# One region of fixed order, index copies behind the first expert's rows, longer planned times for two steps

## The chip, the cores and the metric

The kernel runs on one core of a Trainium2 chip. The metric is the device time of one execution in microseconds, as the median of several runs. The core's engines are TensorE (PE, with its weight loads shown apart as PEld), VectorE (DVE), ScalarE (ACT), GpSimd (POOL) and SyncE (SP); DMA queues carry the transfers.

## What is computed

Attention without a softmax, an RMS norm, and then a mixture of 8 experts in which every token goes to the one expert with the largest logit, up to a capacity. Cut to what matters:

```python
kv = np.einsum('bhsd,bhse->bhde', k, v)              # 8 batches, 8 heads, 576 x 64
out = np.einsum('bhsd,bhde->bhse', q, kv)
x = out / np.sqrt(np.mean(out * out, -1, keepdims=True) + 1e-06) * g_norm   # 4608 tokens x 512
logits = x @ w_gate
expert_idx, gate_w = argmax(logits), softmax(logits)[expert_idx]
# token i goes to the next free slot of its expert, if one is left (cap 1152)
h = np.maximum(np.einsum('ecd,edf->ecf', disp, w1), 0.0)   # 512 -> 1024
y = np.einsum('ecf,efd->ecd', h, w2)                       # 1024 -> 512
out[i] = gate_w[i] * y[expert_idx[i], pos[i]]
```

## The kernel before

**Precision.** Each product is made of three fp16 products: rows and weights are split into a high part and a low part (`xs`, `w1h`/`w1l`, `w2h`/`w2l`, `hh`/`hl`), and high x high, high x low and low x high are added up in fp32.

**Stages.** The attention takes the batches one after the other; its rows go to a table in DRAM, `x_dram` (written at L1050 and L1052), and a routing step ranks each token within its expert. After a few batches the most frequent expert is picked, its weights are loaded, and 384 of its rows (`EARLY`) are worked on beside the rest of the attention. When all batches are through, ten last matmuls (`tab`, L1031, from `rhs`, L1024) finish the table of slots; `read_table` (L1112) turns it into the indices `gidx_tab` (where a slot's row is read) and `sidx_tab` (where its result is written), and `rank_experts` orders the experts by their number of tokens. Then the experts follow by rank, 0 to 7, with `BUDGET` = 704, 672, 640, 624, 592, 576, 560, 544 rows; for rank 0 the 320 rows behind the first 384 are left.

**One expert.** SP loads w1 and w2 in four parts each (`raw`, L341). VectorE takes the largest absolute value of each eighth (`am`, L357); through two small matmuls (`pt_max`, L370 and L377) the largest of all comes back to VectorE, which makes a power of two of it in six small steps (`bmax` to `sg`, L381 to L386: the op `scale`). ScalarE writes the high parts (L391), VectorE the low ones (L397). VectorE copies the expert's six columns of the index table (`slots`, L660; its register load L665, copies `gi` and `si` L669: the op `cut`). GpSimd gathers rows by them, 128 at a time (`xg`, L453, an indirect DMA); `xm` (L461) applies the norm, `gt` (L466) reads the gate weight. Rank 0's rows are turned by TensorE (`xp`, L472), and ScalarE and VectorE write the high and low part of `xs` (L703, L480); from rank 1 on the parts are written to `pair` (L486, L490) and turned by DMA (L494). GEMM1 (`hp`, L557) makes 8 blocks of 128 hidden units, each in one of two PSUM buffers; ScalarE takes the relu (`hh`, L562), VectorE the rest (`hl`, L565), which frees the buffer. `ysc` (L594, L595: the op `scaled`) holds the scale of each result row. GEMM2 (`op` or `yp`, L604) adds up 24 matmuls for a tile of 128 rows, ScalarE writes it out scaled (`ysb`, L629), GpSimd scatters it to DRAM (L634).

**Order.** The kernel doesn't issue in program order. A list scheduler (`Plan`, L107) takes ops with a planned time on an engine, what they depend on, what buffers they take, and a key; at each step it places on the engine that is free first the op with the lowest key among those that are ready. `plan.emit()` then calls them by planned start. So a planned time moves no instruction by itself: it changes when the scheduler thinks that an engine is free. There are two plans. The first holds the attention, the routing and the early 384 rows. The second (from L1525) holds the rest: `weights` (L1540) with `scale` planned at 1.1, `rows_beside` (L1588) with `cut` at 0.4, `products` (L1622) with `scaled` at 1.2, and the loop over ranks at L1678. Each plan is emitted in a region of its own of `manual_schedule`, which keeps each engine's instructions in the order of emission; between the two, at L1344 and L1691, the framework's own scheduler is free to put instructions of one region ahead of those of the other:

Of the kernel before, what the change touches and what calls it, by code (L numbers as in the profile page):

```python
# [26 lines left out]
MANUAL = ("PE", "Activation", "DVE", "Pool", "SP")  # L27
# [17 lines left out]
FIRST = -50.0  # L45
KEY = 10.0
EARLY_TILES = 1
ROWS = 0.0
# [41 lines left out]
class Plan:  # L90
# [5 lines left out]
    def op(self, ways, fn, deps=(), key=0.0, takes=(), uses=()):  # L96

        ways = [ways] if isinstance(ways[0], str) else list(ways)
        o = Op(ways, fn, [d for d in deps if d is not None], list(takes), key)
        for h in takes + uses if isinstance(takes, tuple) and isinstance(uses, tuple) else list(takes) + list(uses):  # L100
            h.users.append(o)
        self.ops.append(o)
        return o
# [56 lines left out]
def attention_moe_kernel(  # L160
# [534 lines left out]
    op = plan.op  # L695
# [420 lines left out]
    early = {}  # L1116
# [224 lines left out]
    order = ExitStack()  # L1341
    order.enter_context(tc.manual_schedule(engines={getattr(mybir.EngineType, e) for e in MANUAL}))
    plan.emit()
    order.close()  # L1344
    actx.close()


# [178 lines left out]
    op = plan.op  # L1526
# [8 lines left out]
    def weights(r, key, after):  # L1535

        ws, sets, zs, holds = wsets[r % 2], [], [], []
        for i in range(2):
            f, z = split_weight(i, ws, (raw1, raw2)[i])
# [8 lines left out]
            for p in range(4):  # L1548
                o = op(("S", 0.43), lambda e, i=i, p=p, regs=regs: load(e, i, p, regs),
                       [regs.get("op"), early["rank"]] + after + (early["free"][p] if r == 1 and i == 0 else []), key,  # L1550
                       (raws[p],))
# [12 lines left out]
            x = new("x")  # L1564
# [5 lines left out]
            o = op(("V", 0.3), lambda e, f=f: f["most"](), tops, FIRST)  # L1570
            o.late = LATE[1] if r > 1 else 0.0
            o = op(("T", 0.12), across, [o], FIRST, (x,))
# [1 line left out]
            o.late = LATE[2] if r > 1 else 0.0  # L1574
            o = op(("T", 0.31), lambda e, f=f, x=x: f["back"](x.t[:, 0:1]), [o], FIRST, (), (x,))
            ew = new(f"e{i}")
            o = op(("V", 1.1), lambda e, f=f, x=x: f["scale"](x.t[:, 0:1]), [o], FIRST, (ew,), (x,))
            zs.append((z, o, ew))
            highs, lows = [], []
            for p in range(8):  # L1580
# [4 lines left out]
            holds.append(hold)  # L1585
        return sets, zs, holds

    def rows_beside(r, key):  # L1588

        hold, sl, st = new("xs"), new("slots"), {}  # L1590

        def cut(e):
            st["gi"], st["si"] = slots(mo, perm_i[0:1, 1, r:r + 1])

        cut_ = op(("V", 0.4), cut, [early["rank"]], key, (sl,))
        n = len(spans(0, BUDGET[r]))
        gates, turned, first, sent = [], [], None, []
        for i in range(n):
            xg, xm, pair = new("xg"), new("xm"), new("pair")

            def fetch(e, i=i):
                if i == 0:
                    st["x"] = Rows(mo, st["gi"], 0, BUDGET[r], BM)
                st["x"].fetch(i)

            o = op(("P", 1.2), fetch, [cut_, first], key, (hold, xg), (sl,))
            first = first or o
            o = op(("D", 0.85), None, [o], key, (), (xg,))
            o.late = 9 if r > 1 else 1.2
            a = op([("P", 1.28), ("V", 0.6)] if r < 3 else ("P", 1.28), lambda e, i=i: st["x"].norm(i, either[e]), [o], key + 1,  # L1610
                   (xm,), (xg,))
            gates.append(op(("V", 0.07), lambda e, i=i: st["x"].gate(i), [o], key + 1, (), (xg, hold)))
            a = op(("A", 0.52), lambda e, i=i: st["x"].pair_high(i), [a], key + 1, (pair,), (xm, hold))
            a = op([("P", 1.37), ("V", 0.66)] if r < 3 else ("P", 1.37), lambda e, i=i: st["x"].pair_low(i, either[e]), [a],
                   key + 1, (), (xm, pair, hold))
            a = op(("S", 1.45), lambda e, i=i: st["x"].pair_turn(i), [a], key + 1, (), (pair, hold))
            sent.append(a)
            turned.append(op(("D", 0.95), None, [a], key + 1, (), (pair, hold)))
            turned[-1].late = 9 if r > 1 else 1
        return st, hold, sl, gates, turned, sent  # L1620

    def products(r, x, xh, xl, gates, xs_hold, si, sl_hold, sets, zs, w_holds, s0, s1):  # L1622
# [32 lines left out]
        def scales(e):  # L1655
            st["g2"] = Gemm2(mo, wsets[r % 2], st["g1"], x().gt, si(), s0, s1)
            st["g2"].scales(y_scale(*[z["e"] for z, _, _ in zs]))

        scaled = op(("V", 1.2), scales, hh[:1] + gates + [o for _, o, _ in zs], urgent, (),
                    (xs_hold, *[x for _, _, x in zs]))  # L1660
        second(r, st, hh, hl, sets and sets[1], scaled, hid, w_holds[1], sl_hold, s0, s1, y_bank)
        return hh
# [5 lines left out]
    def moved(e):  # L1668
# [6 lines left out]
                                              mo, None, lambda: psx.tile([P, 512], F32, tag="x", name="xp"), new("xs"), BM)  # L1675
    args = (lambda st=st: st["rows"], xh, xl, gates, xs_hold, lambda: early["si0"], Hold(None), None, zs, w_holds, EARLY,
            BUDGET[0])
    for r in range(E):  # L1678
        hh = products(r, *args)
        key = KEY * r  # L1680
        if r + 1 < E:
            sets, zs, w_holds = weights(r + 1, key + 1, [] if r > 1 else sent)
            st, xs_hold, sl, gates, turned, sent = rows_beside(r + 1, key + ROWS)
            args = (lambda st=st: st["x"], turned, turned, gates, xs_hold, lambda st=st: st["si"], sl, sets, zs, w_holds, 0,
                    BUDGET[r + 1])
        else:
            op(("P", 9.0), lambda e: nc.gpsimd.drain(), hh[:2], key)
            steps, o = plan_rest(), hh[0]
            for _ in range(60):
                o = op(("V", 0.2), lambda e: next(steps, None), [o], key + 1)  # L1690
    order = ExitStack()  # L1691
    order.enter_context(tc.manual_schedule(engines={getattr(mybir.EngineType, e) for e in MANUAL}))
    plan.emit()
    order.close()
    rest(**table)
# [31 lines left out]
```

## Time and profile before

| what | value |
|---|---|
| median of 3 runs | 574.98 us (573.97 to 575.07) |
| profiled execution | 569.37 us |
| its span, from the first to the last instruction | 567.6 us |
| mean granted TensorE clock | 0.982 |
| TensorE busy | 528.5 us, 93% of the span, 4490 matmuls |
| VectorE busy | 386.8 us, 68% |
| ScalarE busy | 252.6 us, 45% |
| GpSimd busy | 198.9 us, 35% |
| DMA | 102.71 MB, mean 181 GB/s |

The shares are means over stages. In the profile's 40 slices of 14.2 us TensorE is at nine tenths or more nearly everywhere from 184 us on; below that are the first slice (4 tenths), six within the attention (7 or 8), and the two from 156 to 184 us (7), which hold the step from the attention to the experts. So the table says that TensorE is the engine to look at, and the timeline of the slices that are not full says what it waits for. Durations come from the one profiled execution; the span has no launch in it, which is why its own time is 1.8 us longer.

### The profile page before, as it was taken

To read this page: it belongs to the slowest core of one execution; us is meant where nothing else is said; L and a number is where in the kernel's file an instruction comes from. 1 tells how busy PE (TensorE), PEld (TensorE's weight loads), DVE (VectorE), ACT (ScalarE), POOL (GpSimd) and SP (SyncE) were. 2 spreads that over 40 slices of the span, in tenths; PEclk is the share of its full clock that TensorE was granted. 3 is DMA by queue.
4 is the path that set the end of the run, shared out by engine and by line. 5 is a ranking of instruction groups with operands and counts; after the bars stand their busy time and mean duration, and the time that the engine had idled before them with its cause. 6 is when DMAs were issued, how large, how long until landed. Compare 5 with 4: busy or idle time off the path is not lost.

```text
span 567.6 us, 11867 instructions
## 1 busy us (share of the span) xinstructions
PE 528.5 (93%) x4490; PEld 364.6 (64%) x4490; DVE 386.8 (68%) x1072; ACT 252.6 (45%) x490; POOL 198.9 (35%) x244
## 2 busy tenths in 40 slices
PE   4999987978877999999999999999999999999995
PEld 4988876965434576546754674677477558648843
DVE  4387897999838999998999677395848607203800
ACT  1687663886102662655625524253353426212201
POOL 3003335245132471355506431742452375021011
PEclk9999995999999999999999999999999999999998
DMA  8999999662149589699667565583665342010000
GB/s 279 332 357 357 377 383 381 210 257 95 52 150 360 113 250 261 154 308 180 198 160 239 163 153 164 143 172 101 206 159 122 79 102 57 18 55 22 2 37 33
DMA packets 81905, 102.71 MB, mean 181 GB/s; under 512 B 39148, under 2 KB 63724, under 8 KB 80818
## 3 DMA queue, kind: packets, MB, share of 16 engines
q1 hardware_dynamic: 74240, 70.50, 43.3%
q0 software_dynamic: 7584, 31.38, 16.7%
q8 instruction: 37, 0.61, 0.4%
q14 instruction: 26, 0.21, 0.1%
q10 hardware_dynamic: 18, 0.02, 0.0%
HBM read 73.20 MB, written 20.68 MB: 165 GB/s over the span
## 4 chain that ended last, share of the span: by engine, by line
issue 32%; PE 29%; DMA 16%; POOL 13%; DVE 8%; ACT 1%; POOLq 1%; SPq 0%; DVEq 0%
PE hp L557 10%; PE yp L604 9%; DMA v_sb<-in_v_dram 4%; POOL out_dram L634 4%; DMA k_sb<-in_k_dram 4%; POOL pair L490 4%; DMA q_sb<-in_q_dram 3%; POOL xg L453 3%; PE op L823 2%; POOL xm L461 2%; DMA xs<-pair 2%; DVE w1l L397 2%; PE op L557 2%; DMA raw<-in_moe_w_dram 2%; DMA xg<-x_dram,gi 1%
## 5 line engine op out<-in xcount | busy, mean ns | idle before, releaser
L557 PE MATMUL hp<-xs,w1h 128*128 128x320 f16 (+6 forms) x960 | 134.2, 292 | 2.4 <-DVE gt L466 1.2
L557 PEld LDWEIGHTS <-w1h 128*128 128x128 f16 x1024 | 99.4, 98 | 40.0 <-issue 7.3
L634 POOL DMA_INDIRECT out_dram<-ysb,si x42 | 42.9, 1020 | 153.8 <-ACT ysb L629 150.7
L604 PEld LDWEIGHTS <-hh 128*128 128x128 f16 x560 | 54.4, 98 | 63.7 <-issue 1.6
L562 ACT ACTIVATE hh<-hp 128x320 f16<-128x320 f32 (+7 forms) x64 | 41.0, 640 | 108.5 <-PE hp L557 108.5
L357 DVE TENSOR_REDUCE am<-raw 128x1 f32<-128x512 f32 x120 | 75.6, 673 | 4.1 <-DMA raw<-in_moe_w_dram 4.1
L629 ACT ACTIVATE ysb<-yp,ysc 128x512 f32<-128x512 f32 (+5 forms) x41 | 28.1, 685 | 99.9 <-PE yp L604 93.6
L557 PE MATMUL hp<-xs,w1l 128*128 128x320 f16 (+6 forms) x480 | 72.0, 292 | 0.0
L565 DVE SCALAR_TENSOR_TENSOR hl<-hp,hh 128x320 f16<-128x320 f32 (+7 forms) x64 | 47.4, 741 | 32.8 <-ACT hh L562 32.7
L604 PE MATMUL yp<-w2h,hh 128*128 128x512 f16 x272 | 65.3, 379 | 0.8 <-ACT ysb L629 0.8
L604 PE MATMUL yp<-w2l,hh 128*128 128x512 f16 x272 | 65.4, 383 | 0.0
L604 PE MATMUL yp<-w2h,hl 128*128 128x512 f16 x272 | 65.0, 381 | 0.0
L453 POOL DMA_INDIRECT xg<-x_dram,gi x42 | 44.0, 1048 | 49.6 <-DVE gt L466 13.0
L557 PEld LDWEIGHTS <-w1l 128*128 128x128 f16 x512 | 49.8, 98 | 16.3
L823 PE MATMUL op<-kv_bd,qt 128*128 128x144 f32 x320 | 53.0, 301 | 3.5 <-ACT qt L703 2.7
L397 DVE SCALAR_TENSOR_TENSOR w2l<-raw,sw,w2h 128x512 f16<-128x512 f32 x64 | 51.6, 848 | 5.2 <-ACT w2h L391 5.2
L619 DVE COPY yt<-yp 128x256 f32<-128x256 f32 (+4 forms) x7 | 2.9, 412 | 73.4 <-PE yp L613 63.8
L490 POOL TENSOR_TENSOR pair<-xm,pair 128x512 f16<-128x512 f32 (+5 forms) x26 | 34.0, 1308 | 50.3 <-ACT pair L486 50.1
L397 DVE SCALAR_TENSOR_TENSOR w1l<-raw,sg,w1h 128x512 f16<-128x512 f32 x64 | 50.1, 816 | 1.5 <-ACT w1h L391 1.5
L604 PEld LDWEIGHTS <-hl 128*128 128x128 f16 x280 | 27.3, 98 | 32.2 <-issue 1.1
L823 PEld LDWEIGHTS op<-kv_bd,qt 128*128 128x128 f32 x320 | 44.1, 196 | 5.6 <-ACT qt L703 2.9
L391 ACT ACTIVATE w2h<-raw,sw 128x512 f16<-128x512 f32 x62 | 39.7, 710 | 8.1 <-PE yp L613 7.2
(247 smaller groups left out, 698.0 us busy)
## 6 DMA issues: line engine op xcount, KB each, us to landing
raw<-in_moe_w_dram SPq DMA_DIRECT2D x64, 512.0 KB, 5.4
x_dram<-o_sb POOLq DMA_DIRECT2D x8, 720.0 KB, 6.5
k_sb<-in_k_dram SPq DMA_DIRECT2D x16, 320.0 KB, 6.6
v_sb<-in_v_dram SPq DMA_DIRECT2D x16, 320.0 KB, 7.9
q_sb<-in_q_dram SPq DMA_DIRECT2D x16, 320.0 KB, 6.9
x_dram<-o_sb POOLq DMA_DIRECT2D x8, 576.0 KB, 7.4
k_sb<-in_k_dram SPq DMA_DIRECT2D x16, 256.0 KB
v_sb<-in_v_dram SPq DMA_DIRECT2D x16, 256.0 KB, 4.5
```

Source lines behind the costliest of these rows:

```text
L357: nc.vector.tensor_reduce(out=am()[:, p:p + 1], in_=raw[:, sl(p)], axis=AX.X, op=ALU.max, apply_absolute_value=True)
L391: nc.scalar.activation(wh[:, sl(p)], raw[:, sl(p)], AF.Copy, scale=z["s"])
L397: nc.vector.scalar_tensor_tensor(out=wl[:, sl(p)], in0=raw[:, sl(p)], scalar=z["s"], in1=wh[:, sl(p)], op0=ALU.mult, op1=ALU.subtract)
L453: nc.gpsimd.indirect_dma_start(out=self.xg[i][0:n], out_offset=None, in_=x_dram[0:self.rows, :], in_offset=bass.IndirectOffsetOnAxis(ap=se ...
L490: eng.tensor_tensor(out=pair[0:n, 1], in0=self.xm[i][0:n], in1=pair[0:n, 0], op=ALU.subtract)
L557: nc.tensor.matmul(self.view(hp)[:, v], lhsT=w[:, c, f * P:(f + 1) * P], rhs=x[:, c, u * hw:(u + 1) * hw], start=(t == 0 and c == 0), stop ...
L562: nc.scalar.activation(self.out(self.hh, j), self.view(hp), AF.Relu)
L565: nc.vector.scalar_tensor_tensor(out=self.out(self.hl, j), in0=self.view(hp), scalar=0.0, in1=self.out(self.hh, j), op0=ALU.max, op1=ALU.s ...
L604: nc.tensor.matmul(yp[0:n, 0:DM], lhsT=h[:, j, o:o + n], rhs=w[:, j, :], start=(m == 0), stop=(m == len(self.terms) - 1))
L629: nc.scalar.activation(self.ysb[0:n], yp[0:n, 0:DM], AF.Copy, scale=self.ysc[0:n, i:i + 1])
L634: nc.gpsimd.indirect_dma_start(out=(disjoint.pop() if disjoint else out)[:, :], out_offset=bass.IndirectOffsetOnAxis(ap=self.sidx[0:n, col ...
L823: nc.tensor.matmul(ph.t[:, p * 2 * XW:(p + 1) * 2 * XW], lhsT=qt.t[:, (2 * w + p) * P:(2 * w + p + 1) * P], rhs=x, start=True, stop=True)
```

## The change

1. The first plan's region stays open, and the second plan is emitted in the same one (L1344, L1691).
2. The index copies (`cut`) of ranks 2 to 7 depend also on the last low part of rank 0's rows (`placed`, L480 of the 64-row tile), and are planned at 0.9 in place of 0.4.
3. The six steps of a weight scale (`scale`) are planned at 1.4 in place of 1.1 for ranks 2 to 7.
4. The result scales (`scaled`) are planned at 2.4 in place of 1.2 for ranks 1 to 7.

What is computed stays the same.

```diff
@@ -1341,7 +1341,6 @@
     order.enter_context(tc.manual_schedule(engines={getattr(mybir.EngineType, e) for e in MANUAL}))
     plan.emit()
-    order.close()
     actx.close()
...
@@ -1574,7 +1573,7 @@
-            o = op(("V", 1.1), lambda e, f=f, x=x: f["scale"](x.t[:, 0:1]), [o], FIRST, (ew,), (x,))
+            o = op(("V", 1.4 if r > 1 else 1.1), lambda e, f=f, x=x: f["scale"](x.t[:, 0:1]), [o], FIRST, (ew,), (x,))
...
@@ -1585,14 +1584,14 @@
-    def rows_beside(r, key):
+    def rows_beside(r, key, after=()):
...
-        cut_ = op(("V", 0.4), cut, [early["rank"]], key, (sl,))
+        cut_ = op(("V", 0.9), cut, [early["rank"], *after], key, (sl,))
...
@@ -1656,7 +1655,7 @@
-        scaled = op(("V", 1.2), scales, hh[:1] + gates + [o for _, o, _ in zs], urgent, (),
+        scaled = op(("V", 2.4 if r > 0 else 1.2), scales, hh[:1] + gates + [o for _, o, _ in zs], urgent, (),
                     (xs_hold, *[x for _, _, x in zs]))
...
@@ -1675,12 +1674,13 @@
+    placed = xl[-1:]
     for r in range(E):
...
-            st, xs_hold, sl, gates, turned, sent = rows_beside(r + 1, key + ROWS)
+            st, xs_hold, sl, gates, turned, sent = rows_beside(r + 1, key + ROWS, placed if r else ())
...
@@ -1688,8 +1688,6 @@
-    order = ExitStack()
-    order.enter_context(tc.manual_schedule(engines={getattr(mybir.EngineType, e) for e in MANUAL}))
     plan.emit()
     order.close()
```

**TensorE at the end of the early rows.** `op` is the GEMM2 of the first early tile, `yp` that of the later ones, `tab` the last table matmuls. Before, 21 `yp` steps stand between the two (one in three kinds is shown):

```order
L604 MATMUL op<-w2h_175,hl 128x512
L604 LDWEIGHTS hh
L604 MATMUL yp<-w2h_175,hh 128x512
...
L604 LDWEIGHTS hl
L604 MATMUL yp<-w2h_175,hl 128x512
L1031 LDWEIGHTS ohl
L1031 MATMUL tab<-rhs,ohl 128x48
```

After:

```order
L604 MATMUL op<-w2h_175,hl 128x512
L1031 LDWEIGHTS ohl
L1031 MATMUL tab<-rhs,ohl 128x48
...
L604 LDWEIGHTS hh
L604 MATMUL yp<-w2h_175,hh 128x512
```

The ten `tab` stand ahead of all `yp` now; behind them 36 `yp` follow up to the transposes of the first tile of rank 0's rows.

**VectorE at rank 0's last tile of rows.** Before, from the gate of the 64-row tile to its `xm` (three pairs of copies, of which the first is shown whole):

```order
L466 TENSOR_SCALAR gt<-xg 64x1
L665 TENSOR_LOAD perm_i
L665 ISA x2
L669 ISA
L669 COPY gi_2775<-gidx_tab 128x6
L669 ISA
L669 COPY si_2777<-sidx_tab 128x6
...
L461 TENSOR_TENSOR xm<-xg 64x512
L480 TENSOR_TENSOR xs<-xp,xs 128x4x128
```

After:

```order
L466 TENSOR_SCALAR gt<-xg 64x1
L461 TENSOR_TENSOR xm<-xg 64x512
L480 TENSOR_TENSOR xs<-xp,xs 128x4x128
L357 TENSOR_REDUCE am_2773<-raw_172 128x1 x2
L480 TENSOR_TENSOR xs<-xp,xs 128x4x64
L357 TENSOR_REDUCE am_2791<-raw_2628 128x1 x2
L665 TENSOR_LOAD perm_i
L665 ISA x2
L669 ISA
L669 COPY gi_2811<-gidx_tab 128x6
```

The copies of ranks 2 to 5, four pairs that stood between the second tile's gate and the third tile's `xm`, are gone from there. Rank 2's now stand behind rank 0's last low part, those of ranks 3 and 4 within rank 1's GEMM1, of ranks 5 and 6 within its GEMM2.

**VectorE in the first GEMM1 blocks of rank 5.** Before, the second `hl` stands behind a low part of the weights and the scale chain:

```order
L595 TENSOR_SCALAR ysc<-ysc,ys 64x1
L397 SCALAR_TENSOR_TENSOR w2l_176<-raw_2629,sw_5633,w2h_175 128x512
L381 COPY bmax<-pt_max 128x1
L318 TENSOR_SCALAR ew_5991<-bmax 128x1
L319 TENSOR_SCALAR ew_5991<-ew_5991 128x1
L325 TENSOR_SCALAR p2t<-ew_5991 128x1
L327 TENSOR_SCALAR sw_5996<-p2t 128x1
L386 TENSOR_TENSOR sg<-sw_5996,gcol 128x1
L565 SCALAR_TENSOR_TENSOR hl<-hp,hh 128x576
```

After:

```order
L595 TENSOR_SCALAR ysc<-ysc,ys 64x1
L565 SCALAR_TENSOR_TENSOR hl<-hp,hh 128x576
L381 COPY bmax<-pt_max 128x1
L318 TENSOR_SCALAR ew_5999<-bmax 128x1
L319 TENSOR_SCALAR ew_5999<-ew_5999 128x1
L325 TENSOR_SCALAR p2t<-ew_5999 128x1
L327 TENSOR_SCALAR sw_6004<-p2t 128x1
```

The second `hl` stands directly behind `ysc`; the scale chain and the low part follow it. Rank 4 has the same move.

## Rows read from the trace of the kernel before

**Rows 1.** Busy times in two stretches: window, us, busy us (count) by engine, clock, DMA
```profile
168.00:169.00 1.00, 1.00 (x5) 0.69 (x4) 0.40 (x3) 0.15 (x1) 0.75 (x1) 0.50 1.04 359
205.00:262.00 57.00, 57.00 (x419) 33.90 (x416) 54.55 (x110) 24.18 (x39) 24.95 (x23) 1.00 0.91 241
```

**Rows 2.** Timeline from `rhs` to the first gather: start us, us, instruction, [idle before, releaser]
```profile
155.32 1.89 PE L604 MATMUL yp<-w2h,hh 128*128 128x512 f16 x8 [0.78 <-ACT ysb L629]
...
155.39 0.46 DVE L1024 TENSOR_TENSOR rhs<-ohh,tok_hl 128x480 f16<-128x480 f16 x1
...
157.04 1.89 PE L604 MATMUL yp<-w2l,hh 128*128 128x512 f16 x8
...
159.85 0.75 PE L1031 MATMUL tab<-rhs,ohl 128*128 128x48 f16 x10
...
163.06 1.03 POOL L453 DMA_INDIRECT xg<-x_dram,gi  x1 [6.27 <-DVE cmp L1096]
```

**Rows 3.** Timeline from rank 0's first rows to the first GEMM1 of the stage
```profile
166.93 0.69 DVE L461 TENSOR_TENSOR xm<-xg 128x512 f32<-128x512 f32 x1 [2.29 <-issue]
...
167.73 1.08 PE L472 MATMUL xp<-ident,xm 128*128 128x128 f32 x4 [3.89 <-issue]
...
168.60 1.91 PE L604 MATMUL yp<-w2l,hh 128*128 128x512 f16 x4
...
170.50 0.69 DVE L461 TENSOR_TENSOR xm<-xg 128x512 f32<-128x512 f32 x1
...
172.03 1.03 PE L604 MATMUL yp<-w2h,hl 128*128 128x512 f16 x4
172.06 0.15 DVE L466 TENSOR_SCALAR gt<-xg 64x1 f32<-64x1 f32 x1 [0.27 <-DMA xg<-x_dram,gi]
...
172.82 0.17 DVE L669 COPY gi<-gidx_tab 128x6 int32 x1 [0.62 <-issue]
...
174.83 0.68 DVE L461 TENSOR_TENSOR xm<-xg 64x512 f32<-64x512 f32 x1
...
175.57 0.46 PE L472 MATMUL xp<-ident,xm 64*128 64x64 f32 x4 [2.51 <-DVE xm L461]
...
176.48 1.90 PE L557 MATMUL hp<-xs,w1h 128*128 128x320 f16 x12 [0.46 <-ACT xs L703]
```

**Rows 4.** Last write of `x_dram` in the timeline, and its landing in the DMA view
```profile
153.69 0.53 POOL L1050 DMA_DIRECT2D x_dram<-o_sb  x1
...
x_dram<-o_sb POOLq DMA_DIRECT2D x1, 576.0 KB, 5.2
```

**Rows 5.** Timeline: VectorE's `am` ahead of the first `hl`
```profile
177.55 2.45 DVE L357 TENSOR_REDUCE am<-raw 128x1 f32<-128x512 f32 x4
```

**Rows 6.** Timeline: rank 6's index copy amid rank 1's products
```profile
216.58 0.16 DVE L669 COPY gi<-gidx_tab 128x6 int32 x1
```

**Rows 7.** Timeline: GEMM1 of rank 4 (first row) and rank 5
```profile
378.90 1.29 PE L557 MATMUL hp<-xs,w1h 128*128 128x296 f16 x9 [0.29 <-DVE hl L565]
...
424.71 1.35 DVE L595 TENSOR_SCALAR ysc<-ysc,ys 128x4 f32<-128x4 f32 x1
424.85 1.18 POOL L490 TENSOR_TENSOR pair<-xm,pair 128x512 f16<-128x512 f32 x1
...
425.72 0.65 ACT L562 ACTIVATE hh<-hp 128x576 f16<-128x576 f32 x1 [0.35 <-PE hp L557]
...
428.99 0.74 DVE L565 SCALAR_TENSOR_TENSOR hl<-hp,hh 128x576 f16<-128x576 f32 x1
...
429.78 2.12 PE L557 MATMUL hp<-xs,w1h 128*128 128x288 f16 x16 [1.16 <-DVE gt L466]
```

**Rows 8.** Tile views of `xg` (160 to 178 us) and `raw` (160 to 200 us)
```profile
DMA to landing us min/median/max: 3.6/6.4/8.2
...
L341 SPq DMA_DIRECT2D raw<-in_moe_w_dram x8: 346/386/799, 164.9 to 170.5; - x8
...
DMA to landing us min/median/max: 7.4/10.7/14.0
```

## The prediction

> **What bounds the kernel now.** The page's first part comes first: TensorE is busy 93% of the span, VectorE 68%, and no other engine half. The slices of its second part say where TensorE is not full: the start, spots in the attention, and the two slices from 156 to 184 us, at 7 tenths. From there to the end it is nearly full: in the stretch of the second expert it works 57.00 of 57.00 us, with VectorE at 54.55 [rows 1]. So whatever brings the expert stage to an earlier start is gained whole, unless something behind it runs dry; and VectorE has little room there.
>
> Then the timeline of the hole. The last ten table matmuls, `tab`, need `rhs`, done at 155.39 + 0.46 = 155.85, but start at 159.85: TensorE runs 21 `yp` matmuls first [rows 2], as the order in the section on the change shows. All that leads to the first gather hangs on `tab`: it is issued at 163.06, 3.21 us after `tab` starts [rows 2]. The rows then go through VectorE (`xm`), TensorE (`xp`) and ScalarE into the first GEMM1 at 176.48. On that way TensorE idles 3.89, 2.51 and 0.46 us, each time for rows that are not there yet [rows 3]. After the 3.89 us of idling the granted clock is 0.50, the lower level of 1.2 GHz [rows 1]: four `yp` take 1.91 us there and 1.03 later [rows 3].
>
> The last of the three row tiles (64 rows) is the one to watch: its gate is done at 172.06 + 0.15 = 172.21, so its data are there, but its `xm` starts at 174.83. In the 2.62 us between, VectorE makes three pairs of index copies, 0.87 us a pair, most of it idling as before the first, 0.62 us, for no releaser that shows [rows 3].
>
> **The change part by part.** *One region.* With both plans in one region `tab` stands ahead of all `yp`, so it starts at about 155.95 instead of 159.85: 3.9 us. Everything to the first gather follows, since it hangs on nothing else: issue at 159.16. One thing could hold it: the gathers read x_dram, whose last write is issued at 153.69 and lands at most 5.2 us later, at 158.9 [rows 4]. That is 0.3 us ahead; free, but without room. The gathers' spacing stays, so the gates come 3.9 us earlier, the last one ending at 168.31. The 21 `yp` that now lie behind `tab` cost nothing where TensorE would have waited anyway: at 1.72 us for eight (157.04 - 155.32 [rows 2]) the 36 ahead of the first transpose end at 156.6 + 7.7 = 164.3, when the first `xm` (166.93 + 0.69 - 3.9 = 163.7) is done. The transposes of the first tile (0.6 at full clock, an estimate from the 1.08 at half) and eight more `yp` reach 166.7; the second `xm` ends at 170.50 + 0.69 - 3.9 = 167.3 [rows 3], so TensorE waits 0.6 us, far less than the 3.89 that went before the lower clock, and I count full clock.
>
> *Copies.* Behind the last gate stands now the 64-row `xm` itself, at 168.3 instead of 174.83: 6.5 us earlier, of which 3.9 are `tab` and 2.6 the copies. From there to GEMM1 the steps are the same (175.57 to 176.48, 0.91 us), and TensorE's four `yp` behind the second transposes end at about 168.8, before that `xm` ends at 169.0. So GEMM1 starts at about 170.0: **6.5 us**. Its second step, the first `hl`, had four `am` (2.45 us [rows 5]) ahead of it; now two `am` and one pair of copies, half of 2.45 and 0.87, so 2.1: no later. Bounds of this term: from below 2.6 us, if the gathers gain nothing; from above all idle and half-clock time of the stretch, 3.89 + 2.51 + 0.46, 0.88 for those four `yp` and 0.5 for the transposes, 8.2 us [rows 3]. I take 6.5, since the chain of the last tile ends last in both orders.
>
> Copies are not gone. Three pairs (ranks 3, 4, 5) leave idle VectorE time and come to lie between the second expert's products. There VectorE has 2.45 us free in 57 [rows 1]. A copy in such a full queue took 0.16 us without idling [rows 6], so three pairs are 6 x 0.16 = 0.96 us if VectorE sets the pace, and nothing if TensorE does. I take the middle, a **loss of 0.45 us**, for the two are within 5% of each other.
>
> *Planned times of the scales.* In ranks 4 and 5 the second `hl` stood behind the six small steps of the scale chain (L381 to L386) and a `w2l`; TensorE waited for the bank that it frees, 0.29 us at 378.90 and 1.16 us at 429.78 [rows 7]. Now `hl` stands directly behind `ysc`. In rank 5, `ysc` ends at 426.06 (its remainder of 64 rows some 0.3 later), ScalarE's `hh` at 426.37, and `hl` starts at 428.99, so it could come over 2 us earlier: both waits go, **1.45 us**. The chain that moved behind it feeds the `w1h` of the next expert, a GEMM2 away, so the 0.74 us of `hl` put ahead of it are hidden. Bounds: 0, if something else frees the bank as late, to 1.45. I take 1.45, as both inputs of `hl` are there.
>
> Sum: 6.5 + 1.45 - 0.45 = 7.5 us. The profiled execution, 569.37 us (span 567.6 and 1.8 around it), becomes 561.9. It lies 5.6 us under the median of the runs shown, 574.98, from which the same 7.5 give **567.5 us**.
>
> **The rivals.** *R1, VectorE becomes the bound in the second expert.* If each of the three moved pairs keeps its 0.87 us and also waits out a GpSimd step, as `ysc` seems to have done (1.35 us for 128x4, ending when GpSimd's `pair` of 1.18 us ended [rows 7]), they cost 3 x (0.87 + 1.18) = 6.2 us; less the 2.45 free that is 3.8 lost in place of 0.45, and 574.98 - 6.5 - 1.45 + 3.8 = 570.8 us. For it: VectorE's 54.55 of 57. Against it: the copies of 216.58 took 0.16 us in that very stretch. The Trainium skill, "SBUF — State Buffer", section "Who interferes with whom", says that a `copy` may take a pair of ports that VectorE shares with GpSimd and that the later comer blocks fully; by that rule R1 is possible wherever a pair meets a GpSimd step. The trace agrees at `ysc` and not at that copy.
>
> *R2, the gathers do not start earlier*, because x_dram's landing or GpSimd's queue holds them: the room is 0.3 us. Then only the copies' 2.6 and the 1.45 remain: 574.98 - 4.05 = 570.9 us.
>
> *R3, slower: the last gather lands among the weights.* Loads of the second expert's weights hang on the same table and start 3.9 us earlier too. A gather took at most 8.2 us to land, a load up to 14.0, the last one issued at 170.5 and so landing at 184.5 [rows 8]. If the tile of 64 rows comes only when the loads end, at 184.5 - 3.9 = 180.6, GEMM1 starts at 180.6 + 0.15 + 0.7 + 0.06 + 0.91 = 182.4, 5.9 us later than now; with 1.45 gained, 579.4 us. It is slower by over 0.2% (1.15 us, about what a measurement of this kernel can tell) once that gather lands later than about 177.3, some 15 us after its issue at 161.7. Against it: gathers and loads start in the same distance as before, where it took 6.4.
>
> *R4, no change:* the lead is given back, because the rows or weights of the second expert come no earlier. Its first gather follows `tab` by 3.9, the later ones follow the buffers that the 64-row `xm` frees, by 6.5; so little speaks for it. Time: 575.
>
> **How the numbers follow.** Forecast 0.65, R1 0.16, R2 0.09, R3 0.05, R4 0.05. Range: upwards R1, R2 and the scale term at 0 on top of them (570.9 + 1.45 = 572.4), so 572.5; downwards the upper bound of the first term, 8.2 + 1.45 = 9.65 and so 565.3, rounded to 565.0. That leaves out R3 and R4. Faster by over 0.2% are the forecast, R1 and R2: 0.90; within, 0.05; slower, 0.05.
>
> **What would show it.** In the changed profile: `tab` right behind `rhs` and ahead of `yp`; first gather near 159.2; no copies between the last gate and the 64-row `xm`; first GEMM1 near 170.0; granted clock 1.00 throughout the hand-over; no wait of TensorE over 0.25 us at the second `hl` of ranks 4 and 5; the second expert's stretch still without idling. I am wrong if the first GEMM1 starts near 174 (R2), if TensorE begins to wait for VectorE between it and the third expert (R1), or if a gate waits past 170 for its gather (R3).

## The result and the profile after

| | before | changed |
|---|---|---|
| median | 574.96 us (573.97 to 575.07, 4 runs) | 566.78 us (566.29 to 567.92, 4 runs) |
| ratio | | 0.9864, 95% interval 0.9846 to 0.9883 |
| span of the profiled execution | 567.6 us | 564.5 us |

The change makes the kernel 8.2 us faster in this comparison: 566.78 us, where 567.5 was predicted. But the two profiled spans differ by 3.1 us only, so the first question is which of the two is the change. In three comparisons the changed kernel stood at 0.9864, 0.9896 and 0.9874 of the kernel before; the second and the third were made on different chips (numbers 13 and 14; that of the first is not on record), and the medians of before were 574.96, 570.57 and 573.42 us. The last two make it 6.4 and 6.5 us. One execution of before beside the third took 696.45 us at a mean clock of 0.751 and is left out of its ratio. The profiled execution of before (569.37 us) lies below all its four timed runs in the first comparison and amid those of the second; so what is compared below are runs timed beside each other, their ratios, or profiles measured from a common event.

The first page lines of the changed kernel, busy times and the 40 slices of TensorE:

```profile
span 564.5 us, 11863 instructions
## 1 busy us (share of the span) xinstructions
PE 527.8 (94%) x4490; PEld 363.0 (64%) x4490; DVE 390.3 (69%) x1071; ACT 252.0 (45%) x490; POOL 201.2 (36%) x245
...
PE   5999977878879999999999999999999999999995
```

The slice from 169 us on is at nine tenths now, the one before it still at 7. The hand-over itself, from the timeline of the changed kernel (start us, us, instruction, idle before and its releaser):

```profile
154.32 0.53 POOL L1050 DMA_DIRECT2D x_dram<-o_sb  x1
...
156.01 0.46 DVE L1024 TENSOR_TENSOR rhs<-ohh,tok_hl 128x480 f16<-128x480 f16 x1
...
156.53 0.75 PE L1031 MATMUL tab<-rhs,ohl 128*128 128x48 f16 x10 [1.36 <-DVE rhs L1024]
...
158.71 0.17 DVE L669 COPY gi<-gidx_tab 128x6 int32 x1 [0.57 <-issue]
...
160.95 1.02 POOL L453 DMA_INDIRECT xg<-x_dram,gi  x1 [3.54 <-DVE perm L1105]
...
161.61 7.04 SPq L341 DMA_DIRECT2D raw<-in_moe_w_dram  x8
...
166.19 0.69 DVE L461 TENSOR_TENSOR xm<-xg 128x512 f32<-128x512 f32 x1 [4.59 <-DMA xg<-x_dram,gi]
...
166.98 0.63 PE L472 MATMUL xp<-ident,xm 128*128 128x128 f32 x4 [1.93 <-issue]
...
168.49 1.91 PE L604 MATMUL yp<-w2h,hl 128*128 128x512 f16 x4
...
170.18 0.15 DVE L466 TENSOR_SCALAR gt<-xg 64x1 f32<-64x1 f32 x1 [1.16 <-DMA xg<-x_dram,gi]
...
171.29 0.68 DVE L461 TENSOR_TENSOR xm<-xg 64x512 f32<-64x512 f32 x1 [0.97 <-PE xp L472]
...
173.36 1.79 PE L557 MATMUL hp<-xs,w1h 128*128 128x320 f16 x12 [0.64 <-ACT ysb L629]
```

`rhs` itself ends 0.62 us later than in [rows 2], before any part of the change acts; so everything is counted from its end, 156.47. `tab` follows at once, as forecast. But the first gather is issued 4.48 us behind `rhs`, where 3.31 were forecast (159.16 - 155.85), and 2.24 behind the start of its index copy, where the kernel before had 1.04 (163.06 - 162.02): it waits for something that is not its index. The releaser that the row names, `perm`, has nothing to do with a gather; it is only the last one that happened to end before. And the first `xm` starts 5.24 us after the issue (166.19 - 160.95), where it was 3.87 (166.93 - 163.06). From `rhs` to the first GEMM1 it is 16.89 us, against 20.63 before. The rows of the kernel before for the index copy and the first weight load:

```profile
162.02 0.17 DVE L669 COPY gi<-gidx_tab 128x6 int32 x1 [0.56 <-issue]
...
164.93 5.97 SPq L341 DMA_DIRECT2D raw<-in_moe_w_dram  x8
```

The two waits in ranks 4 and 5 are gone; TensorE's rows at the places of [rows 7] carry no idle time, and the second `hl` of rank 5 starts 0.35 us behind the big `ysc` (its 1.35 us of length are still there):

```profile
376.53 2.18 PE L557 MATMUL hp<-xs,w1h 128*128 128x296 f16 x16
...
422.34 1.35 DVE L595 TENSOR_SCALAR ysc<-ysc,ys 128x4 f32<-128x4 f32 x1
...
424.04 0.76 DVE L565 SCALAR_TENSOR_TENSOR hl<-hp,hh 128x576 f16<-128x576 f32 x1
...
426.09 2.12 PE L557 MATMUL hp<-xs,w1h 128*128 128x288 f16 x16
```

### The profile page after: what moved, and what is told of

It reads as the page before. It is cut to its first block, busy times and chain, and to the rows that moved or that the text cites. A ratio compares the mean times of both kernels' runs of the same rounds, so it can differ in the third digit from the quotient of the medians.

```text
span 564.5 us, 11863 instructions
## 1 busy us (share of the span) xinstructions
PE 527.8 (94%) x4490; PEld 363.0 (64%) x4490; DVE 390.3 (69%) x1071; ACT 252.0 (45%) x490; POOL 201.2 (36%) x245
## 4 chain that ended last, share of the span: by engine, by line
PE 36%; issue 29%; DMA 11%; POOL 11%; DVE 9%; ACT 2%; SPq 1%; another core or an unknown queue 1%; POOLq 0%; ACTq 0%
PE yp L604 13%; PE hp L557 12%; DMA q_sb<-in_q_dram 4%; POOL out_dram L634 4%; POOL pair L490 3%; PE op L823 2%; DMA k_sb<-in_k_dram 2%; POOL xg L453 2%; PE op L557 2%; DMA raw<-in_moe_w_dram 2%; POOL xm L461 2%; DMA v_sb<-in_v_dram 1%; DMA xs<-pair 1%; PE qp L805 1%; DVE w2l L397 1%
## 5 line engine op out<-in xcount | busy, mean ns | idle before, releaser
L397 DVE SCALAR_TENSOR_TENSOR w2l<-raw,sw,w2h 128x512 f16<-128x512 f32 x64 | 53.8, 877 | 2.6 <-ACT w2h L391 2.6
L397 DVE SCALAR_TENSOR_TENSOR w1l<-raw,sg,w1h 128x512 f16<-128x512 f32 x64 | 51.4, 839 | 0.7 <-ACT w1h L391 0.7
L461 POOL TENSOR_TENSOR xm<-xg 128x512 f32<-128x512 f32 (+5 forms) x33 | 39.2, 1188 | 16.3 <-DVE pair L490 13.1
```

The source lines that it names most:

```text
L397: nc.vector.scalar_tensor_tensor(out=wl[:, sl(p)], in0=raw[:, sl(p)], scalar=z["s"], in1=wh[:, sl(p)], op0=ALU.mult, op1=ALU.subtract)
L461: eng.tensor_tensor(out=self.xm[i][0:n].rearrange("p (h d) -> p h d", h=H), in0=xg[:, :, 0:D], in1=xg[:, :, D:D + 1].broadcast_to([n, H, D ...
```

## The experiments

One table first, from the timelines of all profiles, so that each part can be read by its own stage. Columns G to E are in us and come from one profiled execution of each kernel. G: issue of the first gather behind the end of `rhs`. T: end of the 64-row gate, likewise. M: start of the first GEMM1, likewise. S: from there to the first GEMM1 of rank 3, three experts. E: from there to the start of TensorE's last matmul. Before again, one region, copies alone and planned times alone ran on chip 1; the changed kernel again, copies and times, x_dram by SyncE and late weights on chip 13; the changed kernel a third time and the last three rows on chip 14.

| kernel | G | T | M | S | E | ratio to before |
|---|---|---|---|---|---|---|
| before | 7.21 | 16.36 | 20.63 | 139.99 | 244.51 | |
| before, again | 7.20 | 16.58 | 21.09 | 141.75 | 244.51 | 1.0002 (0.9974 to 1.0030) |
| one region alone | 4.98 | 15.40 | 19.70 | 140.87 | 244.50 | 0.9991 (0.9965 to 1.0017) |
| copies alone | 7.19 | 16.28 | 18.15 | 141.79 | 244.64 | 0.9976 (0.9951 to 1.0000) |
| planned times alone | 7.20 | 16.41 | 20.69 | 140.57 | 242.97 | 0.9972 (0.9945 to 0.9999) |
| copies and times | 7.20 | 16.41 | 18.00 | 140.23 | 242.97 | 0.9912 (0.9889 to 0.9935) |
| changed | 4.48 | 13.86 | 16.89 | 140.96 | 243.89 | 0.9864 (0.9846 to 0.9883) |
| changed, again | 4.35 | 14.87 | 16.47 | 143.17 | 242.97 | 0.9896 (0.9862 to 0.9930) |
| changed, third | 4.57 | 13.80 | 15.39 | 141.05 | 243.88 | 0.9874 (0.9851 to 0.9897) |
| changed, x_dram by SyncE | 4.61 | 14.16 | 15.75 | 142.94 | 242.97 | 0.9878 (0.9839 to 0.9916) |
| changed, late weights | 4.13 | 10.90 | 13.49 | 142.58 | 242.98 | 0.9852 (0.9822 to 0.9883) |
| late weights, two regions | 7.20 | 14.39 | 17.88 | 142.15 | 243.89 | 0.9889 (0.9869 to 0.9910) |
| late weights, late am (5) | 3.59 | 10.75 | 13.07 | 143.02 | 243.87 | 0.9793 (0.9770 to 0.9817) |
| late weights, late am (4) | 5.22 | 11.99 | 14.81 | 148.18 | 243.84 | 0.9843 (0.9819 to 0.9866) |

**The kernel before, again.** No edit.

> The kernel before, unchanged, profiled and timed once more. Between the two profiled executions shown so far the change is worth 3.1 us (spans 567.6 and 564.5), between the medians 8.2 us. Theory H1 (the prediction's sum): the single executions scatter, the 8 us are steps that add up, and a second profile of before lies anywhere between 568 and 576 us, with the rows of the hand-over (last table matmuls to first GEMM1 of the expert stage, 16.6 us) the same within 1 us. Theory H2: the timed executions of before contain some 5 us that the first profile lacks, in one place; a second profile then shows either 569 us again or about 575 us, and in the latter case one stretch that is longer by about 5 us. Ratio 1.000 by both.

Thirty-five executions of before beside the first four kernels lie between 567.16 and 574.97 us, with a median of 570.41; so single executions scatter by 7.8 us. The second profile (span 570.3 us) shows one source. Its windows of the hand-over and of the first GEMM1 blocks (busy us by engine, then clock, DMA share, GB/s):

```profile
164.00:176.00 12.00, 5.62 (x22) 2.60 (x20) 5.43 (x24) 1.86 (x3) 5.35 (x6) 0.85 0.84 271
176.00:182.00 6.00, 5.29 (x22) 3.18 (x23) 4.68 (x9) 0.52 (x2) 3.03 (x3) 0.50 1.03 394
```

With the idle time of 2.73 us ahead of the last transposes the clock fell a second time, and the first GEMM1 ran at 0.50, 1.2 GHz, up to 182.5. The first profile of before had one such stretch in the hand-over, 3.5 us long [rows 1]; this one has two, 3.4 and some 7 us. The mean clock of the 35 executions goes with their time: the six fastest (567.2 to 568.4 us) lie at 0.982 to 0.984, the six slowest (572.1 to 575.0) at 0.974 to 0.977. So differences of 5 us arise between executions without any step of the kernel. In the two profiles M and E are the same within 0.5 us, as H1 has it; S differs by 1.8, and most of the second low stretch lies in it. The runs of 574 to 575 us beside the result were not profiled, so that they are slow for the same reason is likely, not shown.

**One region alone.**

```diff
     plan.emit()
-    order.close()
     actx.close()
...
-    order = ExitStack()
-    order.enter_context(tc.manual_schedule(engines={getattr(mybir.EngineType, e) for e in MANUAL}))
     plan.emit()
     order.close()
```

> Only the first edit: both plans in one region; the copies and the planned times as before. The table matmuls then stand ahead of all yp, but the three pairs of copies stay between the gate of the 64-row tile and its xm. H1: 3.9 us faster, so a ratio of 0.993. H2 (most of the gain in the medians hangs on the order of the table matmuls, through something that the first profile of before did not show): 6 us or more, ratio 0.990 or less. A third reading, that the copies alone held the last tile, gives under 1 us.

It is worth 1 us in the medians (569.44 against 570.41), and its interval includes no change. `tab` starts as early as it should. The timeline shows where the lead goes:

```profile
158.90 0.17 DVE L669 COPY gi<-gidx_tab 128x6 int32 x1 [0.56 <-issue]
...
161.67 1.02 POOL L453 DMA_INDIRECT xg<-x_dram,gi  x1 [4.05 <-DVE cmp L1107]
161.79 5.54 SPq L341 DMA_DIRECT2D raw<-in_moe_w_dram  x8
...
164.26 0.91 POOL L453 DMA_INDIRECT xg<-x_dram,gi  x1 [0.30 <-issue]
...
171.94 0.15 DVE L466 TENSOR_SCALAR gt<-xg 64x1 f32<-64x1 f32 x1 [2.26 <-DMA xg<-x_dram,gi]
...
175.47 0.46 PE L472 MATMUL xp<-ident,xm 64*128 64x64 f32 x4 [4.68 <-DVE xm L461]
```

The gather comes 2.77 us behind its copy, at the same moment as the weight loads, and the gate of the last tile starts 7.68 us after that tile's gather (171.94 - 164.26), where it was 6.41 before (172.06 - 165.65). This led to theory L: the first gather waits for the landing of x_dram's last write, while the loads, which do not, move up to it, and the gathers share the DMA engines with 4 MB of weights.

**Copies alone.**

```diff
-        cut_ = op(("V", 0.4), cut, [early["rank"]], key, (sl,))
+        cut_ = op(("V", 0.9), cut, [early["rank"], *after], key, (sl,))
```

(and `placed` handed to it, as in the change)

> Only the second edit: the copies of ranks 2 to 7 behind rank 0's last low part and planned at 0.9; two regions, planned times of the scales as before. The 21 yp stay ahead of the table matmuls. H1: 2.6 us faster, ratio 0.9955. H2: 1 us or less in the medians if the 5 us sit in the order of the table matmuls; 5 us or more if they sit in the copies.

At the first GEMM1 it gives what was forecast: M falls by 2.7 us from the mean of the two profiles of before (20.86), for a T that stays. (Of the four moved pairs, three stood between the last gate and the last `xm`; rank 2's, at 168.69 in the kernel before, stood ahead of the second gate.) The median falls by 1.9 us only, and the interval reaches to no change. The timeline shows two new waits of TensorE, in ranks 1 and 2, each for an `hl` that now stands behind low parts of the weights:

```profile
212.55 1.73 PE L557 MATMUL hp<-xs,w1h 128*128 128x336 f16 x11 [1.35 <-DVE hl L565]
...
277.90 1.38 PE L557 MATMUL hp<-xs,w1h 128*128 128x320 f16 x9 [0.93 <-DVE hl L565]
```

**Planned times alone.**

```diff
-            o = op(("V", 1.1), lambda e, f=f, x=x: f["scale"](x.t[:, 0:1]), [o], FIRST, (ew,), (x,))
+            o = op(("V", 1.4 if r > 1 else 1.1), lambda e, f=f, x=x: f["scale"](x.t[:, 0:1]), [o], FIRST, (ew,), (x,))
...
-        scaled = op(("V", 1.2), scales, hh[:1] + gates + [o for _, o, _ in zs], urgent, (),
+        scaled = op(("V", 2.4 if r > 0 else 1.2), scales, hh[:1] + gates + [o for _, o, _ in zs], urgent, (),
```

> Only the third and fourth edits: scale planned at 1.4 and scaled at 2.4; two regions, copies as before. The second hl of ranks 4 and 5 then stands directly behind ysc. H1: 1.45 us faster, ratio 0.9975, and TensorE's waits of 0.29 and 1.16 us there are gone. H2: the same; if the 5 us sit in these waits in the timed executions, 5 us or more.

1.76 us faster, and column E is the cleanest number of the study: 242.97 against 244.51, twice, so 1.54 us, with 1.45 forecast. The remaining 0.2 are inside the scatter. Edits 3 and 4 were not tried apart.

**The changed kernel, again, and copies and times without the region.** The first has no edit, the second is the change without its first edit.

> The changed kernel once more, beside more runs of before. In 35 runs beside the first four kernels, before lay between 567.2 and 575.0 us with a median of 570.4; the four shown with the result (574.0 to 575.1) are its upper end. By the profiles the parts are worth 3.7 us from rhs to the first GEMM1 and 1.5 us in ranks 4 and 5. If the rest of the 8.2 us was scatter (theory S), the gain is 5.2 us: about 565.2 us, ratio 0.991. If the sum of the prediction holds in the median (theory H1), 7.5 us: about 563, ratio 0.987.

> The second, third and fourth edits without the first: two regions, so the 21 yp stay ahead of the table matmuls. Theory L (with one region the first gather waits for the landing of x_dram's last write, and its rows come among the weights; so the region is worth 1 us of the 3.9): 2.6 + 1.5 = 4.1 us faster than before, ratio 0.993, and no waits of 1.5 us at rank 1 and 1.1 at rank 2 as with the copies alone, if the longer planned times took them away. Theory H1: 7.5 - 3.9 = 3.6 us, ratio 0.994, and 3.9 behind the changed kernel beside it; by L only 1 us behind it.

Changed again: 564.21 against 570.57, 6.4 us, between the two readings. Copies and times: 565.36, so 5.2 us without the region, more than the 4.1 of theory L; the region adds 1.2 in the medians beside it, as L has it; H1 wanted 3.9, which the two intervals together (0.9862 to 0.9930 and 0.9889 to 0.9935) hardly leave room for. By the medians, copies and times are worth more together than apart (0.9912, against 0.9976 x 0.9972 = 0.9948 on another chip): of the two waits that the copies made, the one of rank 2 is gone and that of rank 1 is shorter:

```profile
216.20 2.44 PE L557 MATMUL hp<-xs,w1h 128*128 128x336 f16 x16 [0.78 <-DVE gt L466]
```

That the longer time for `scaled` did this is likely, but not shown by itself, since edits 3 and 4 always came together.

The second profile of the changed kernel shows x_dram's landing, in its DMA view and its timeline:

```profile
x_dram<-o_sb POOLq DMA_DIRECT2D x1, 576.0 KB, 5.4
```

```profile
153.31 0.53 POOL L1050 DMA_DIRECT2D x_dram<-o_sb  x1
...
159.82 1.02 POOL L453 DMA_INDIRECT xg<-x_dram,gi  x1 [3.42 <-DVE perm_i L1104]
160.60 6.62 SPq L341 DMA_DIRECT2D raw<-in_moe_w_dram  x8
...
214.62 1.58 PE L557 MATMUL hp<-xs,w1h 128*128 128x336 f16 x10 [0.78 <-DVE gt L466]
...
239.73 0.38 PE L377 MATMUL pt_max<-bm,ones 1*128 1x1 f32 x2 [0.90 <-DVE bm L374]
...
271.01 1.26 PE L557 MATMUL hp<-xs,w1h 128*128 128x320 f16 x8 [1.15 <-DVE hl L565]
```

153.31 + 5.4 = 158.7, and the gather's row starts 1.1 us later. That is about the distance from the start of the index copy to the gather where the copy was last (162.02 to 163.06, 1.04). The trace also records the updates of the semaphore by which a write reports its landing, and the first gather waits for that semaphore. Its last update lies 1.12 us ahead of the gather in all three profiles of the changed kernel (159.83 and 160.95 in the first), and 1.13 in that of the region alone (160.54 and 161.67). So landing plus 1.1 is the gate. The last three rows show what the prediction named as the sign of rival R1, in one execution: TensorE waits for VectorE in ranks 1 and 2, and S is 143.17, against 140.96 and 141.05 in the two other profiles of the changed kernel.

**Late weights.** SyncE reads the second expert's number from a copy made behind the first gate (`held`, on which the loads depend), so its loads start after the first gather has landed, at 164.09, 10.0 us behind `rhs` in place of 5.1:

```diff
-                    regs["e"] = nc.sync.value_load(perm_i[0:1, 0, r:r + 1], min_val=0, max_val=E - 1)
+                    regs["e"] = nc.sync.value_load(perm_j[0:1, 0:1] if r == 1 else perm_i[0:1, 0, r:r + 1], min_val=0, max_val=E - 1)
...
+    held = op(("V", 0.1), lambda e: nc.vector.tensor_copy(perm_j[0:1, 0:1], perm_i[0:1, 0, 1:2]), gates[:1], FIRST)
```

> The changed kernel with the second expert's weight loads held back: SyncE reads the expert's number from a copy that VectorE makes behind the first gate of rank 0's rows, so no load starts before the first gather has landed. Theory L (contention): the gathers land 3.6 to 4.2 us after their issue in place of 5.2 to 6.6, and the 64-row xm starts by 2 us earlier against rhs. What the later loads then cost VectorE, whose am wait for them, is open: total between 2 us faster and 4 us slower than the changed kernel. If the loads do not delay the gathers, these still take over 5 us.

The view of the tile `xg` over the three gathers of rank 0 (157 to 162 and 158 to 163 us; the landing of the second is in neither), of this kernel and then of the changed one, again:

```profile
DMA to landing us min/median/max: 3.3/3.5/3.6
```

```profile
DMA to landing us min/median/max: 4.5/6.1/7.8
```

That is the contention shown: the first and the third gather land in 3.6 and 3.3 us without the weights beside them, and in 4.5 and 7.8 with them. The Trainium skill, "DMA: Bandwidth & Descriptors", section "Queues, rings and completion order", says that a DMA engine serves its queues in turns, a packet at a time; by that a small gather shares every engine with the large loads, and these rows agree, though none shows the turns themselves. M falls by another 3 us from the changed kernel beside it, to 13.49 (by 1.9 to 3.4 from its three profiles). The first gather itself is still held by the write: 1.12 us behind the last update, at 157.07. Part of it is handed back at once, since an `am` that waits for a late load now stands ahead of the first `hl`:

```profile
172.68 0.69 DVE L357 TENSOR_REDUCE am<-raw 128x1 f32<-128x512 f32 x1 [2.63 <-DMA raw<-in_moe_w_dram]
...
173.81 1.25 PE L557 MATMUL hp<-xs,w1h 128*128 128x320 f16 x8 [2.85 <-DVE p2t L325]
```

Still 561.78 us, 2.4 faster than the changed kernel beside it, a little beyond the better end of what was expected; the two intervals overlap.

**x_dram by SyncE.** The last batch's two writes are issued on SyncE's queue.

```diff
-                    nc.gpsimd.dma_start(rows[:, 0:C], o_sb[0:P:2].rearrange("p c h x -> p c (h x)"))
+                    (nc.sync if b == NB - 1 else nc.gpsimd).dma_start(rows[:, 0:C], o_sb[0:P:2].rearrange("p c h x -> p c (h x)"))
```

(and the other write likewise)

> The changed kernel with the last batch's two writes of x_dram issued on SyncE's queue in place of GpSimd's; the order of every other engine is the same. Theory L: the first gather, which now starts 4.5 us behind rhs, waits for that landing; if the hardware queue lands it sooner, the gather starts up to 1.2 us earlier (3.3 us behind rhs, set by the index copy), lies further ahead of the loads, and lands within about 4.2 us; first GEMM1 up to 2 us earlier against rhs: ratio to before 0.003 lower than that of the changed kernel. If something else holds the gather, the issue stays at 4.5 us and the time the same.

A miss: the landing is no shorter (6.2 us in its DMA view, against 5.4 of the changed kernel, again, and 5.2 to 6.2 in the other profiles that show it), and the gather stays at 4.61 behind `rhs`, 0.8 behind the landing. The ratio differs from the changed kernel's by less than the intervals. As the landing did not move forward, the run does not test what an earlier landing would give; it says only that the other queue did not bring one, in one profile.

**Late weights with later `am`, and with two regions.**

```diff
-LATE = (4.0, 2.0, 1.0, 2.0)
+LATE = (4.0, 2.0, 1.0, 5.0)
```

> The kernel with the late weight loads, and the plan told that the second expert's loads land 5 us after their planned transfer in place of 2 (the last entry of LATE), so that no am stands ahead of the first hl. With the late loads alone the first GEMM1 came 13.5 us behind rhs (16.5 and 16.9 in the changed kernel), and then TensorE lost 3.0 us at its third block, behind an hl that stood behind an am. Theory: those 3.0 us go, and at most half of them come back where the am lie now, as VectorE is nearly full up to the third expert: 1.5 to 3 us faster than with the late loads alone, ratio to before 0.980 to 0.983. If VectorE sets the pace there as a whole, nothing: 0.985.

> The kernel with the late weight loads, but with two regions again, so that the 21 yp stand ahead of the table matmuls. Theory L: with the loads out of the way of the gathers the region is worth what the first gather gains against rhs, 7.2 - 4.1 = 3.1 us at the first GEMM1, not the 1 us that it was worth among the loads; part of it may be lost up to the third expert. So 1.5 to 3 us slower than with the late loads in one region: ratio 0.988 to 0.991. If the region is worth the same with and without the loads, 1 us: 0.987.

> As the kernel with the late loads and the later am, with 4 us in place of 5: one am still stands ahead of the first hl. Theory: that am waits for a load again, less long than before, so TensorE loses 0 to 1.5 us at the third block, in place of 3.0 and of nothing: ratio 0.981 to 0.985.

> The changed kernel a third time, on the chip of the three others, so that they stand beside it. From the two comparisons so far (ratios 0.986 and 0.990): 0.988, and between 562 and 568 us in single executions.

With 5 us: 561.71 against 573.42, and 566.96 for the changed kernel beside it. It is the fastest version of the study, 11.7 us under before and 5.3 under the change, whose third comparison came out at 0.9874, with 0.988 expected. The wait at the third block is gone, and by the ratios the gain on the late weights alone is 3.4 us, measured on another chip, where 1.5 to 3 were expected. But it is not the `am` alone: `LATE` is also used for the first expert's loads during the attention, so its end is ordered otherwise. x_dram's last write is issued 3.2 us ahead of the start of `rhs` in place of 1.7, and its last update, at 155.68, comes level with the index copy:

```profile
155.66 0.17 DVE L669 COPY gi<-gidx_tab 128x6 int32 x1 [0.56 <-issue]
...
156.81 1.02 POOL L453 DMA_INDIRECT xg<-x_dram,gi  x1 [1.95 <-DVE rank L1098]
```

So the write holds the gather back by 0.1 us at most, and G is 3.59, close to the 3.31 of the forecast: this is where one region puts the first gather when the write lands in time. How much of the gain is the `am` and how much the attention's end was not separated. With 4 us the order falls out worse. The write lands late again (last update at 156.52, gather 1.07 behind it), and G is 5.22. There is no wait at the third block of rank 0 either, against what was expected; TensorE waits 1.77 us for the weights' maximum (1.87 with 5 us), and 2.76 in rank 1 for an `hl` behind three low parts (0.57 at the same block with 5 us). Behind these 2.76 us the granted clock is 0.50 for some 3 us (209 to 212 us), and S is 148.18. So one step of a planner's constant is worth 3.8 us through orders that nobody chose.

With two regions the late weights give 0.9889, against 0.9852 with one, on another chip: 2.1 us, where L wanted 1.5 to 3 and its rival 1; the intervals just overlap. M differs by 4.4 us (17.88 and 13.49), and TensorE's wait at the third block is shorter here (1.16 against 2.85), which gives part of it back.

## Why the prediction was right, and where it was not

**The sum.** 7.5 us forecast, 8.2 in the first comparison, 6.4 and 6.5 in two more. The size came out right, the mechanism in part. The term of the region was far too large: 3.9 us forecast, 1.0 to 1.2 measured in the medians. What made up for it was not in the sum and is not explained (see what stays open), so that the total came so near is in part luck. The prediction's own signs say the same: in the first profile the first gather came at 160.95 and not near 159.2, the first GEMM1 at 173.36, nearer to R2's 174 than to 170.0, and in all three profiles of the changed kernel the last gate waits past 170 for its gather, R3's sign, if narrowly (170.18, 170.20 and 170.85; counted from `rhs`, only the second is past it).

**One region, 3.9 us: too large.** The step that failed is "That is 0.3 us ahead; free, but without room". The landing at 158.9 was right, but it was held against the start of the gather's row, 159.16. The gather starts 1.1 us after that landing, so the gate was at 160.0 and the gather 0.8 late; measured G is 4.35 to 4.57 against 3.31, as the write took 5.4 to 5.6 us to land in the changed kernel, in place of 5.2. Next, "gathers and loads start in the same distance as before" was wrong for the same reason: the loads kept their lead and the gather did not, so the distance shrank from 1.87 us (164.93 - 163.06) to 0.66 (161.61 - 160.95). That is rival R2 in part and the beginning of rival R3; the late weights show R3's mechanism to be real, at some 3 us and not at the size that R3 gave it.

**Copies, 2.6 us: right** at the first GEMM1, 2.7 alone, of which the median showed 1.9. In the first profile of the changed kernel something took a part of their place: `xm` of the last tile waits 0.97 us for its buffer, which the second transposes free late (171.29, released by `xp`).

**Both together, 6.5 us at the first GEMM1: 4.6 measured** (20.86 as the mean of two profiles of before, 16.25 as the mean of three of the changed kernel, which lie between 15.39 and 16.89).

**Full clock: not so in every execution.** TensorE idled 1.93 us ahead of the first transposes, not 0.6, as the gathers were late; in the first profile of the changed kernel the clock was low again from 168.2 to 171.4:

```profile
168.00:171.00 3.00, 3.00 (x11) 1.57 (x9) 1.16 (x4) 0.23 (x1) 1.41 (x2) 0.52 0.91 321
```

In the two others it stayed at 1.00 there (164 to 176 us of the second):

```profile
164.00:176.00 12.00, 8.45 (x54) 5.12 (x54) 7.63 (x23) 3.10 (x6) 4.50 (x5) 1.00 1.01 358
```

The two profiles of before have one and two such stretches. Beside each other, executions of before have mean clocks of 0.973 to 0.982 and the changed kernel 0.983 to 0.987 in the second comparison, and 0.975 to 0.983 against 0.979 to 0.986 in the third. So less idling seems to buy clock as well, a gain that the sum had left out; its share was not separated from the rest.

**Scales, 1.45 us: right**, 1.54, and shown alone.

**Moved copies, 0.45 us lost: not resolved.** S against the mean of before (140.87) is +0.1, +0.2 and +2.3 us, and the two profiles of before differ by 1.8 themselves. The prediction's reading of `ysc`, that the trace agrees with the Trainium skill's rule on the port that VectorE shares with GpSimd ("SBUF — State Buffer", "Who interferes with whom"), needs a correction. By that rule the later comer is blocked. In the changed kernel `ysc` takes 1.17 us for 128x5 at 208.50 and ends at 209.67, as GpSimd's `xm` (208.53) ends at 209.63; so the two are held together, but `ysc` starts first by the rows, as it does in [rows 7], and the rows do not show it as the later comer. The moved copies took 0.16 each (215.27 in the second profile), so they are not what the waits in the second profile came from. What did it stays open: the order of instructions is the same in all three profiles, and the one that reached the first GEMM1 earliest (15.39) has no such waits. The two kernels with M of 13.1 to 13.5 have an S of 142.6 and 143.0, so a part of a larger lead may be handed back there.

**What stays open.** By the means of the profiles the change is worth 4.6 (M) - 0.9 (S) + 0.9 (E) = 4.7 us, or 5.2 with the 1.5 that E shows where it is cleanest; by the medians it is 6.4 to 8.2. One execution of a kernel is one draw of 5 us and more of scatter, and the difference was not traced. On some profiles, in the kernels of both kinds of order, TensorE has waits of 0.2 to 0.7 us within the turned GEMM2 (L613) for no releaser that shows, and a column E that is 0.9 us longer: the first profile of the changed kernel and all four from chip 14 have them, those from chips 1 and 13 don't. The first profile of before hasn't got them either. They go with the chip, it seems, which wasn't tried; if so, the first two profiles, of before and of the changed kernel, come from different chips.

## What to carry to other kernels

Before a step is credited with its lead, every other input of the next step is to be put on the same axis, and at the same point: the landing of a write plus the time from a release to the start of the instruction, not the landing alone. A chain that is pulled forward brings its neighbours along, and if one neighbour is held and another is not, they meet: here the loads met the gathers, and holding the loads back by 5 us gave 2.4 in the medians, more than the region that had brought them together. And a planned time is a promise about order for every later op: the copies' edit alone made two new waits further on, and with the longer times of the scales beside it one was gone and the other shorter.

## What was not expected of the hardware

Executions of one kernel on one chip differ by 7.8 us of 570, with mean TensorE clocks of 0.971 to 0.984. After TensorE had idled for 1.3 to 2.9 us the clock fell in some executions and not in others: in the changed kernel it fell behind 1.93 us in one profile and not behind 1.84 in another, and it fell behind 2.76 us with the late `am` (4) and not behind 2.85 with the late weights alone. In the second profile of before it fell a second time, for some 7 us. Two gathers of rank 0 land in 3.3 and 3.6 us by themselves, and in 7.8 and 4.5 beside the weight loads. The first gather starts 1.1 us after the landing of the GpSimd-issued write that it waits for, 0.8 after that of the SyncE-issued one. The queue from which 1.3 MB are written did not bring them to land sooner: 6.2 us after the issue of the last write from SyncE's, 5.2 to 6.2 from GpSimd's.
